# Bias rows added on VectorE, one DMA of rows per chunk, and a new order of work in a fused attention and MLP kernel

## The chip, the cores and the metric

The kernel runs on one core of a Trainium2 chip. The metric is device time in microseconds (us) of one launch; the smaller the better. The core has several engines that run their own instruction streams: TensorE (PE in the profile; PEld is its weight load), VectorE (DVE), ScalarE (ACT), GpSimd (POOL) and SyncE (SP). SyncE, ScalarE and GpSimd also issue DMAs. Every engine works through its instructions strictly in the order in which the program gives them, and waits where an instruction needs something that is not there yet.

## The reference

One input `x` of 2048 rows and 640 columns (bf16) is normalised, and the result goes through two independent branches whose outputs are added to `x`:

```python
xn = layernorm(x)
# A: 32 heads of 20; each position attends to itself and 7 earlier ones, 2 apart
q, k, v = split(xn @ wqkv)
logits = sum_d(q[s] * k[s - 2*w]) * 20**-0.5          # w = 0..7, masked before the start
o = sum_w(softmax(logits)[s, w] * v[s - 2*w]) @ wo
# B: MLP with 1536 hidden units
h = gelu(xn @ w1 + b1) @ w2 + b2
out = x + o + h
```

The change is about the terms `x` and `b2` of the last line, and about the order in which everything is done.

## The kernel before

**Tiling.** The 2048 rows are 16 blocks of 128 (numbers 0 to 15) in 4 chunks of 512 rows (n = 0 to 3; a block has the number bl = 0 to 3 in its chunk). A chunk goes through these stages, each of which is a `do_...` function that issues the instructions of one task:

- `st`, `rs`, `rc`, `xn` (lines 373 to 410): statistics and normalisation of a block, then `tp` and `tc` (412 to 424): transposition on TensorE and a copy to SBUF.
- `pj`/`pc` (438, 475): q, k and v of a chunk, TensorE and a cast on ScalarE. Chunk 0 does this by block with `gj`/`gc`.
- `qk` (488): products q times shifted k on VectorE, eight of 128x2560 elements. `lg` (500): TensorE sums them over a head.
- `m`, `mx`, `ex`, `ss`, `ri`, `at` (525 to 567): the softmax, VectorE and one exponential on ScalarE.
- `xd` and `xs` (569 to 581): the "expansion". The softmax weights `attn`, one row per head, are spread by DMA over the partitions into the tile `ax`, two DMAs issued by SyncE and two by ScalarE.
- `av` (584): eight products v times weights (`pv`) on VectorE; `ad` and `ot` add them up to the tile `oT`.
- `f1`/`ge` (606, 618): the hidden layer, TensorE and the GELU on ScalarE, into 12 tiles `hT`.
- `o` (626): the output of one block, in five pieces `pc` 0 to 4: four of three hidden tiles each, and a last one with `oT` and `wo`. Each weight tile is used for 512 columns into the PSUM tile `lo` and 128 columns into `hi`. Chunks 0 to 2, and blocks 12 and 14 of the last chunk, use one PSUM pair that only one block can hold; blocks 13 and 15 use two of the four `acc` tiles.
- `oc` (647): two casts on ScalarE to the bf16 tile `osb`, of which there are two.
- `od` (653): the block goes to the output by a DMA that GpSimd issues.

**x and b2.** Line 328 loads `b2` into every partition (`b2bc`). Line 330, in SyncE's queue behind all loads, copies the first 15 blocks of `x` from DRAM to the output in DRAM. For each of these blocks `od` then issues two DMAs on GpSimd's queue that add to what the output holds: `b2bc` (line 656) and the computed block (657). The first kind of all blocks runs right after the copy.

Block 15 (`LASTB`) has no such addition. `xb` (426) adds `b2bc` to its rows of `x_sb` on VectorE, and `o` adds the result with a matmul against the identity (line 637). Its 512 wide columns are done first ("lo" only, in five pieces), then cast by `oclo` and stored by a plain DMA of SyncE (666). `ohi` (668) does the 128 narrow columns with 18 matmuls; `ochi` (672) casts on VectorE, and ScalarE issues the store (675).

**The order.** Nothing above is issued in the order of the loops. `make_plan` (149) adds each task with an engine, an assumed duration, a rank, what it needs, the buffers that it holds and, for some, an earliest time. `Plan.run` (57) then walks through time: when an engine is free it takes, among the tasks that are ready and whose buffers fit, the one with the lowest rank. The tasks are issued in the order of their start times in that walk, and this is the order of every engine's stream. The rank is worked out from the chunk (`base` is 52 n, and `early` is `base` - 85, or - 37 for chunk 1), plus the offset of its name in the table `RANK` (141), which is looked up by the first three letters of the name, four for names with "pj", "pc" and "ad". A lower rank goes first. The durations and the walk are assumptions of the program; on the chip the engines take as long as they take, in that fixed order.

The rank of block bl of chunk n is `base` + 60 + 8 bl, and that of `ohi` is 156 + 142 = 298, each plus its offset.

Of the kernel before, what the change touches and what calls it, by code (L numbers as in the profile page):

```python
# [11 lines left out]
ALU = mybir.AluOpType  # L12
# [3 lines left out]
PE, VE, SE, DQ = "pe", "ve", "se", "dq"  # L16


class Plan:
# [101 lines left out]
S, D, F, H, W, DIL = 2048, 640, 1536, 32, 8, 2  # L121
P = 128
DH = D // H
PAD = (W - 1) * DIL
KT, FT = D // P, F // P
CH = 512
NCH = S // CH
BPC = CH // P
# [5 lines left out]
LASTB = S // P - 1  # L134
# [4 lines left out]


RANK = {
# [4 lines left out]
}  # L146


def make_plan(fns, offsets=RANK):

    pl = Plan(offsets)
# [6 lines left out]
    def f(kind, *a):  # L158
        return lambda: fns[kind](*a)

    def done(n, which):
        if n:
            return [f"pc{n}{which}{to}" for to in range(KT)]
        return [f"gc{bl}{g}" for bl in range(BPC) for g, parts in enumerate(GROUPS) if which in [p[0] for p in parts]]

    for n in range(NCH):
        base = n * PERIOD
        prev = base - PERIOD
        early = base + (-37.0 if n == 1 else -85.0)
# [11 lines left out]
            pl.add(f"rc{n}", VE, 0.25, early + -4.0, [f"rs{n}"], f("rstd", n, 0, BPC))  # L181
        for bl in range(BPC):
            xn, tp = ("xn", n, bl), ("acc", "tp", n, bl)
            pl.add(f"xn{n}{bl}", SE if n else VE, 0.65 if n else 0.42, early + -4.0 if n else -99, [f"rc{n}" if n else f"rc{n}{bl}"], f("xn", n, bl), [xn])
            pl.add(f"tp{n}{bl}", PE, 0.3, early + -3.0 if n else -99, [f"xn{n}{bl}"], f("tp", n, bl), [xn, tp])
            pl.add(f"tc{n}{bl}", SE, 0.65, early + -3.0 if n else -99, [f"tp{n}{bl}"], f("tc", n, bl), [tp, xnT])
        if n == NCH - 1:
            pl.add("xb", VE, 0.5, base + 36, [f"xn{n}{BPC - 1}"], f("xb"), after=31.0)

        if n == 0:  # L190
            for bl in range(BPC):
                for g, parts in enumerate(GROUPS):
                    ps, last = ("acc", "g", bl, g), max(p[0] for p in parts)
# [5 lines left out]
        for which, buf in enumerate((q, k, v)):  # L199
# [5 lines left out]
            if which:  # L205
                need = done(n - 1, which) if n else []
# [3 lines left out]
        L = ("L", n)  # L210
        for wp in range(W // 2):
            pr = ("prod", "qk", n, wp)
            for i in range(2):
                need = done(n, 0) + done(n, 1) + [f"pad{n}1"]
                pl.add(f"qk{n}{wp}{i}", VE, 1.42, base + 3.0 * wp + i, need, f("qk", n, wp, i), [q, k, pr])
            pl.add(f"lg{n}{wp}", PE, 0.6, n - 1000, [f"qk{n}{wp}{i}" for i in range(2)] + ([f"lg{n}{wp-1}"] if wp else []), f("lg", n, wp), [pr, L], slack=0.8)

        e, at, ax = ("e", n), ("attn", n), ("ax", n)
        m, rs, ss, z = ("m", n), ("rs", n), ("ss", n), ("prod", "z", n)
# [4 lines left out]
        pl.add(f"ri{n}", VE, 0.96, n - 1000, [f"ss{n}"], f("recip", n), [ss, rs])  # L224
        pl.add(f"at{n}", VE, 1.22, n - 1000, [f"ri{n}"], f("attn", n), [e, rs, at])
        pl.add(f"xs{n}", SE, 1.2, n - 1000, [f"at{n}"], f("xs", n), [at, ax])
        pl.add(f"xd{n}", DQ, 5.5, n - 1000, [f"at{n}"], f("xd", n), [at, ax])

        prs = [("prod", "av", n, wp) for wp in range(W // 2)]
        for wp in range(W // 2):  # L230
            for i in range(2):
                need = [f"xd{n}", f"xs{n}", f"pad{n}2"] + done(n, 2)
                pl.add(f"av{n}{wp}{i}", VE, 1.42, base + 15.0 + 6.0 * wp + i, need, f("av", n, wp, i), [v, ax, prs[wp]])
        for k2, (a, b, r) in enumerate(((0, 1, 9.0), (2, 3, 21.0), (0, 2, 22.0))):
            need = [f"av{n}{x}{i}" for x in (a, b) for i in range(2)] if k2 < 2 else [f"ad{n}0", f"ad{n}1"]
# [8 lines left out]
        for bl in range(BPC):  # L244
            ob = ("osb", n, bl)
            O = [("O", n, bl)] if n < NCH - 1 or bl % 2 == 0 else [("acc", "lo", n, bl), ("acc", "hi", n, bl)]
            final = n * BPC + bl == LASTB
            last = None
            for pc in range(5):
                need = [last] if last else [f"ge{n}{ft}" for ft in range(FT)] + (["xb"] if (n, bl) == (NCH - 1, BPC - 1) else [])  # L250
                if pc == 4:
                    need.append(f"ot{n}")
                us = (0.65, 0.65, 0.65, 0.87, 1.08)[pc] if final else (0.82, 0.82, 0.82, 0.82, 1.37)[pc]
                last = pl.add(f"o{n}{bl}{pc}", PE, us, base + PERIOD + 8.0 + 8.0 * bl, need, f("o", n, bl, pc, ("lo",) if final else ("lo", "hi")), O + (hTs if pc == 0 else hTs[3 * pc : 3 * pc + 3] if pc < 4 else [oT]), 31.0)
            if final:
                pl.add("oclo", SE, 0.55, base, [last], f("oclo"), O + [ob])
                last = pl.add("ohi", PE, 1.05, base + PERIOD + 90, [last], f("ohi"), O)
                pl.add("ochi", VE, 0.25, base, [last], f("ochi"), O + [ob])
                continue
            pl.add(f"oc{n}{bl}", SE, 0.78, base, [last], f("oc", n, bl), O + [ob])  # L260
            pl.add(f"od{n}{bl}", SE, 0.0, base, [f"oc{n}{bl}"], f("od", n, bl), [ob])
# [4 lines left out]
def kernel(  # L266
# [16 lines left out]
    nc = tc.nc  # L283
    assert tuple(A_x.shape) == (1, S, D) and tuple(B_w1.shape) == (D, F)

    x_sd = A_x.rearrange("b s d -> (b s) d")
    out_sd = out.rearrange("b s d -> (b s) d")
# [18 lines left out]
    x_sb = wts.tile([P, NCH * BPC, D], BF16, name="x_sb")  # L306
# [5 lines left out]
    b2bc = consts.tile([P, D], BF16, name="b2bc")  # L312
# [9 lines left out]
    for n in range(1, NCH):  # L322
        cs = slice(n * BPC, (n + 1) * BPC)
# [2 lines left out]
    nc.sync.dma_start(w2_sb[:], B_w2.rearrange("(t p) n -> p t n", p=P))  # L326
    nc.sync.dma_start(wo2[:], A_wo.rearrange("(p t) n -> p t n", t=KT))  # L327
    nc.sync.dma_start(b2bc[:], b2_bcast)  # L328

    nc.sync.dma_start(out_sd[0 : LASTB * P, :], x_sd[0 : LASTB * P, :])  # L330


    ident = consts.tile([P, P], BF16, name="ident")
# [89 lines left out]
            tiles["tp", n, bl][:, 0 : KT * P].rearrange("p (t m) -> p t m", t=KT),  # L423
        )

    def do_xb():
        nc.vector.tensor_tensor(out=x_sb[:, LASTB, :], in0=x_sb[:, LASTB, :], in1=b2bc[:], op=ALU.add)


    def qkv_tile(n, which):  # L430
# [222 lines left out]
    def do_od(n, bl):  # L653
        b = n * BPC + bl
        rows = out_sd[b * P : (b + 1) * P, :]
        nc.gpsimd.dma_start(rows, b2bc[:], accum_op=ALU.add)  # L656
        nc.gpsimd.dma_start(rows, tiles["osb", n, bl][:], accum_op=ALU.add)  # L657


    last = (NCH - 1, BPC - 1)  # L660
# [18 lines left out]
    with tc.manual_schedule(engines=engines):  # L679

        idle = psA.tile([P, CH], F32, tag="acc", name="idle")
        for _ in range(WARM):
            nc.tensor.matmul(idle[:, 0:P], lhsT=ident[:], rhs=ident[:], start=True, stop=True)
        for t in make_plan(fns).run():
            t["fn"]()
# [30 lines left out]
```

## Time and profile before

| | us |
|---|---|
| median of 3 runs | 227.08 |
| lowest and highest run | 226.92 and 228.39 |
| the profiled execution | 227.29 |
| its span, first to last instruction | 225.0 |
| TensorE busy in it | 212.4 |
| VectorE busy | 175.3 |
| ScalarE busy | 115.7 |
| GpSimd busy | 27.8 |

How to read the profile's lines. A line of the timeline has the start, the duration (both us, from the span's start), the engine, the line of the kernel, the operation, the tiles (result <- operands), the shapes and how many instructions are put together; in brackets stands how long the engine was idle before it and what ended that. An engine name with a q behind it is that engine's issuing of a DMA or its semaphore work. In a line of the slices, the span is cut into 40 equal parts, and each digit is the busy share in tenths. A line of the groups has the count, the busy time in us and the mean duration in ns, then the idle time before. A line of the DMA issues has the size of one and the time from issue to landing. A line of one source line's instructions has lowest, median and highest duration in ns, and the first and the last start.

### The profile page before, as it was taken

How to read it: one execution, taken by the hardware profiler on the slowest of the kernel's cores; microseconds unless marked ns; L12 is line 12 of the kernel's file. 1: busy time of each engine (PE TensorE's matmuls, PEld its weight loads, DVE VectorE, ACT ScalarE, POOL GpSimd, SP SyncE). 2: the span in 40 equal slices, each digit the busy share in tenths (PEclk: the TensorE clock that was granted, in tenths of full speed). 3: DMA queues.
4: the chain of work that ended last, by engine and by line, in shares of the span. 5: the costliest groups of instructions: out<-in, count | busy, mean ns of one | idle time of the engine just before them, and what ended most of it. 6: DMA issues, size and time to landing. Idle time of an engine off the chain costs nothing.

```text
span 225.0 us, 4057 instructions
## 1 busy us (share of the span) xinstructions
PE 212.4 (94%) x1728; PEld 123.2 (55%) x1754; DVE 175.3 (78%) x166; ACT 115.7 (51%) x203; POOL 27.8 (12%) x48
## 2 busy tenths in 40 slices
PE   6899999999996999999999999999999999999990
PEld 6799745555443555555555555555445455455550
DVE  3759997567399998999899999999998229995000
ACT  3675988887674746923277542221548431511220
POOL 2000004990000000101010001111100110101111
PEclk9999999999999999999999999999999999999998
DMA  6999992999300000227001422222200532202322
GB/s 228 366 368 389 378 468 42 155 171 198 92 0 0 3 0 0 32 39 179 0 3 26 97 92 29 29 32 31 32 0 0 109 110 29 29 3 29 54 29 35
DMA packets 13625, 21.98 MB, mean 98 GB/s; under 512 B 1144, under 2 KB 10744, under 8 KB 13560
## 3 DMA queue, kind: packets, MB, share of 16 engines
q1 hardware_dynamic: 7848, 14.52, 19.7%
q0 software_dynamic: 4320, 4.92, 16.9%
q10 hardware_dynamic: 1440, 2.29, 3.2%
q8 instruction: 13, 0.21, 0.4%
q14 instruction: 4, 0.03, 0.0%
HBM read 12.45 MB, written 7.54 MB: 89 GB/s over the span
## 4 chain that ended last, share of the span: by engine, by line
issue 71%; POOL 10%; SPq 9%; DMA 7%; POOLq 1%
DMA out_dram<-in_A_x_dram 7%; POOL out_dram L657 5%; POOL out_dram L656 5%; SPq L327 4%; SPq L324 2%; SPq L326 1%; SPq L325 1%; SPq L318 1%; SPq L321 0%; POOLq L711 0%; SPq L320 0%; SPq L328 0%; SPq L315 0%; POOLq L657 0%; POOLq L656 0%
## 5 line engine op out<-in xcount | busy, mean ns | idle before, releaser
L610 PE MATMUL hps<-xnT,w_sb 128*128 128x512 bf16 x234 | 55.2, 380 | 0.3
L588 DVE TENSOR_TENSOR pv<-vT,ax 128x2560 bf16<-128x2560 bf16 x32 | 45.9, 1485 | 12.2 <-DMA ax<-attn 12.1
L643 PE MATMUL lo<-w_sb,hT 128*128 128x512 bf16 x183 | 52.2, 380 | 0.0
L493 DVE TENSOR_TENSOR prod<-qT,kT 128x2560 bf16<-128x2560 bf16 x32 | 45.8, 1486 | 3.1 <-ACT kT L478 2.8
L621 ACT ACTIVATE hT<-hps,b1T 128x512 bf16<-128x512 f32 x48 | 31.9, 688 | 19.7 <-PE hps L610 14.4
L645 PE MATMUL hi<-w_sb,hT 128*128 128x128 bf16 x192 | 40.3, 219 | 0.6 <-issue 0.2
L610 PEld LDWEIGHTS <-w_sb 128*128 128x128 bf16 x240 | 22.4, 98 | 26.2 <-issue 1.5
L597 DVE TENSOR_TENSOR pv<-pv 128x5120 bf16<-128x5120 bf16 x12 | 33.8, 2822 | 0.2
L657 POOL DMA_DIRECT2D out_dram<-osb x15 | 12.9, 863 | 157.0 <-ACT osb L651 157.0
L650 ACT CAST osb<-lo 128x512 bf16<-128x512 f32 x15 | 8.8, 587 | 45.6 <-PE hi L645 29.6
L643 PEld LDWEIGHTS <-hT 128*128 128x128 bf16 x192 | 18.7, 98 | 22.5 <-issue 0.4
L643 PE MATMUL lo<-wo,oT 128*128 128x512 bf16 x76 | 22.4, 380 | 0.0
L645 PEld LDWEIGHTS <-hT 128*128 128x128 bf16 x192 | 18.3, 98 | 2.1
L656 POOL DMA_DIRECT2D out_dram<-b2bc x15 | 13.5, 2696 | 35.1 <-DMA out_dram<-in_A_x_dram 35.1
L443 PE MATMUL pps<-xnT,wq_sb 128*128 128x512 bf16 x72 | 17.5, 381 | 0.2
L443 PE MATMUL pps<-xnT,wk_sb 128*128 128x512 bf16 x74 | 17.3, 379 | 0.2
L645 PE MATMUL hi<-wo,oT 128*128 128x128 bf16 x80 | 16.9, 219 | 0.2
L443 PE MATMUL pps<-xnT,wv_sb 128*128 128x512 bf16 x72 | 16.7, 380 | 0.3 <-ACT xnT L421 0.2
L478 ACT CAST qT<-pps 128x512 bf16<-128x512 f32 x15 | 8.8, 588 | 11.5 <-PE pps L443 11.5
L505 PE MATMUL L<-prod,head_of 128*32 128x256 bf16 x320 | 11.7, 275 | 2.1 <-DVE prod L493 2.1
L376 DVE BATCH_NORM_STATS2 stats<-x_sb 128x6 f32<-128x320 bf16 x16 | 7.4, 462 | 7.1 <-DMA x_sb<-in_A_x_dram 7.1
L399 ACT ACTIVATE xn<-x_sb,nmr,rstd 128x640 bf16<-128x640 bf16 x12 | 10.8, 921 | 4.0 <-PE tp L417 4.0
(68 smaller groups left out, 217.2 us busy)
## 6 DMA issues: line engine op xcount, KB each, us to landing
w_sb<-in_B_w_dram SPq DMA_DIRECT2D x2, 1920.0 KB, 16.4
out_dram<-in_A_x_dram SPq DMA_DIRECT2D x1, 2400.0 KB
out_dram<-b2bc POOLq DMA_DIRECT2D x15, 160.0 KB, 7.3
out_dram<-osb POOLq DMA_DIRECT2D x15, 160.0 KB, 3.4
ax<-attn SPq DMA_DIRECT2D x8, 256.0 KB, 5.3
ax<-attn ACTq DMA_DIRECT2D x8, 256.0 KB, 6.6
x_sb<-in_A_x_dram SPq DMA_DIRECT2D x3, 640.0 KB, 11.4
wq_sb<-in_A_wqkv_dram SPq DMA_DIRECT2D x1, 800.0 KB, 4.7
```

The source lines that it names most:

```text
L399: nc.scalar.activation(xn[:], x_sb[:, b, :], ACT.Identity, bias=nmr[:, b : b + 1], scale=rstd[:, b : b + 1])
L443: nc.tensor.matmul(ps[:], lhsT=wqkv_p[which][:, ti, to, :], rhs=xnT[:, ti, :], start=(ti == 0), stop=(ti == KT - 1),)
L493: nc.vector.tensor_tensor(out=prod[:, i, :, :], in0=qkv_tile(n, 0)[:], in1=qkv_tile(n, 1)[:, :, off : off + CH], op=ALU.mult,)
L505: nc.tensor.matmul(L[j * H : (j + 1) * H, 2 * wp : 2 * wp + 2, :], lhsT=head_of[:], rhs=prod[:, :, t, j * P : (j + 1) * P], start=(t == 0 ...
L588: nc.vector.tensor_tensor(out=pv[:, i, :, :].rearrange("p t (j c) -> p t j c", j=BPC), in0=qkv_tile(n, 2)[:, :, off : off + CH].rearrange( ...
L597: nc.vector.tensor_tensor(out=ta[:], in0=ta[:], in1=tb[:], op=ALU.add)
L610: nc.tensor.matmul(ps[:], lhsT=w1_sb[:, ti, ft * P : (ft + 1) * P], rhs=tiles["xnT", n][:, ti, :], start=(ti == 0), stop=(ti == KT - 1),)
L621: nc.scalar.activation(hT[:], tiles["hps", n, ft][:], ACT.Gelu_apprx_tanh, bias=b1T[:, ft : ft + 1], scale=1.0)
L643: nc.tensor.matmul(lo[:], lhsT=lhs, rhs=rhs[:, 0:CH], start=first, stop=last)
L645: nc.tensor.matmul(hi[:, 0 : D - CH], lhsT=lhs, rhs=rhs[:, CH:D], start=first, stop=last)
L656: nc.gpsimd.dma_start(rows, b2bc[:], accum_op=ALU.add)
L657: nc.gpsimd.dma_start(rows, tiles["osb", n, bl][:], accum_op=ALU.add)
```

## The change

1. The copy of `x` to the output (line 330) is removed, and so is the accumulating DMA of `b2bc` in `od` (line 656).
2. `xb` is now a task of every chunk: one VectorE addition of `b2bc` to the chunk's four blocks of `x_sb`, in place, then one DMA on SyncE's queue that writes these rows to the output (for the last chunk without block 15). It needs the chunk's normalised blocks, and every output block of the chunk needs it in the plan. GpSimd's remaining accumulating DMA adds the computed block to these rows.
3. The plan's durations of `xn`, `lg` and `xd` are raised, and `RANK` is another table, and so the order of all engines is another.

```diff
 RANK = {
-    "ad01": -51.8, "ad02": -11.1, "ad22": 55.2, "av0": -75.4, "av1": -80.6, "av2": 15.4, "f10": 39.3, "f11": 0.8,
-    "f12": 46.1, "f13": 9, "ge1": -74.9, "gj3": 24.7, "o00": 64.8, "o01": 58, "o02": 58.8, "o21": 9.1,
-    "o30": 13.6, "o32": -88, "o33": -87.4, "pc10": 184.3, "pc12": -37.1, "pj21": -29.9, "qk1": -33.9, "qk2": -278.2,
-    "qk3": -4, "st2": 95.7, "tc1": -44.4, "tp2": 50.9, "tp3": -44.5, "xb": 57, "xn1": 17.4, "xn2": 19.4,
+    "av0": 264.6, "av1": 32, "f10": -2, "f11": 10.6, "f12": 127.1, "f13": 83.2, "gj2": -18.9, "gj3": -1.6,
+    "o00": 26.6, "o02": 3.7, "o03": -5.9, "o22": 138.2, "o33": 95.3, "pad": 1.2, "pj22": 202, "pj32": 66.6,
+    "qk2": 13.5, "rc3": 115.5, "st2": 183.2, "tc1": -1, "tp3": -99.8, "xb3": 226, "xn2": 124, "xn3": 8.8,
 }
...
-            pl.add(f"xn{n}{bl}", SE if n else VE, 0.65 if n else 0.42, early + -4.0 if n else -99, [f"rc{n}" if n else f"rc{n}{bl}"], f("xn", n, bl), [xn])
+            pl.add(f"xn{n}{bl}", SE if n else VE, 0.81 if n else 0.42, early + -4.0 if n else -99, [f"rc{n}" if n else f"rc{n}{bl}"], f("xn", n, bl), [xn])
...
-        if n == NCH - 1:
-            pl.add("xb", VE, 0.5, base + 36, [f"xn{n}{BPC - 1}"], f("xb"), after=31.0)
+        pl.add(f"xb{n}", VE, 1.43, base + 36, [f"xn{n}{bl}" for bl in range(BPC)], f("xb", n), after=32.0)
...
-            pl.add(f"lg{n}{wp}", PE, 0.6, n - 1000, [f"qk{n}{wp}{i}" for i in range(2)] + ([f"lg{n}{wp-1}"] if wp else []), f("lg", n, wp), [pr, L], slack=0.8)
+            pl.add(f"lg{n}{wp}", PE, 0.65, n - 1000, [f"qk{n}{wp}{i}" for i in range(2)] + ([f"lg{n}{wp-1}"] if wp else []), f("lg", n, wp), [pr, L], slack=0.8)
...
-        pl.add(f"xd{n}", DQ, 5.5, n - 1000, [f"at{n}"], f("xd", n), [at, ax])
+        pl.add(f"xd{n}", DQ, 6.0, n - 1000, [f"at{n}"], f("xd", n), [at, ax])
...
-                need = [last] if last else [f"ge{n}{ft}" for ft in range(FT)] + (["xb"] if (n, bl) == (NCH - 1, BPC - 1) else [])
+                need = [last] if last else [f"ge{n}{ft}" for ft in range(FT)] + [f"xb{n}"]
...
-    nc.sync.dma_start(out_sd[0 : LASTB * P, :], x_sd[0 : LASTB * P, :])
...
-    def do_xb():
-        nc.vector.tensor_tensor(out=x_sb[:, LASTB, :], in0=x_sb[:, LASTB, :], in1=b2bc[:], op=ALU.add)
+    def do_xb(n):
+        cs = slice(n * BPC, (n + 1) * BPC)
+        nc.vector.tensor_tensor(
+            out=x_sb[:, cs, :],
+            in0=x_sb[:, cs, :],
+            in1=b2bc[:].unsqueeze(1).to_broadcast([P, BPC, D]),
+            op=ALU.add,
+        )
+        cs = slice(n * BPC, min((n + 1) * BPC, LASTB))
+        nc.sync.dma_start(out_sd.rearrange("(b p) d -> p b d", p=P)[:, cs, :], x_sb[:, cs, :])
...
     def do_od(n, bl):
         b = n * BPC + bl
         rows = out_sd[b * P : (b + 1) * P, :]
-        nc.gpsimd.dma_start(rows, b2bc[:], accum_op=ALU.add)
         nc.gpsimd.dma_start(rows, tiles["osb", n, bl][:], accum_op=ALU.add)
```

## The prediction

> **What bounds the kernel now.** I read the page's busy times and slices first, then who waited for whom, then the timeline of the two places where TensorE is idle.
>
> ```profile
> PE 212.4 (94%) x1728; PEld 123.2 (55%) x1754; DVE 175.3 (78%) x166; ACT 115.7 (51%) x203; POOL 27.8 (12%) x48
> PE   6899999999996999999999999999999999999990
> DVE  3759997567399998999899999999998229995000
> ```
>
> TensorE is busy for 212.4 of 225.0 us. Counted from 0, only slices 0 and 1, slice 12 (67.5 to 73.1 us) and slice 39 are under nine tenths. So a change pays by the time at which TensorE ends, or by what follows that. The profiled execution took 227.29 us, 2.26 more than its span; the median of the runs is 227.08, 0.2 lower.
>
> The end of the timeline, then the landing times of the outputs and the closing instructions:
>
> ```profile
> 209.13 1.24 PE L643 MATMUL lo<-wo,oT 128*128 128x512 bf16 x5
> 210.46 0.59 ACT L665 CAST osb<-lo 128x512 bf16<-128x512 f32 x1 [0.38 <-ACT osb L651]
> 211.07 0.35 SPq L666 DMA_DIRECT2D out_dram<-osb  x1
> 213.20 0.38 PE L643 MATMUL lo<-w_sb,hT 128*128 128x512 bf16 x1
> 217.82 0.83 PE L645 MATMUL hi<-w_sb,hT 128*128 128x128 bf16 x12
> 218.54 0.44 PE L645 MATMUL hi<-wo,oT 128*128 128x128 bf16 x5
> 218.57 0.59 ACT L650 CAST osb<-lo 128x512 bf16<-128x512 f32 x1 [3.82 <-DMA out_dram<-osb]
> 219.06 0.27 ACT L651 CAST osb<-hi 128x128 bf16<-128x128 f32 x1
> 219.08 0.29 DVE L674 CAST osb<-hi 128x128 bf16<-128x128 f32 x1 [13.47 <-PE hi L645]
> 219.40 0.36 ACTq L675 DMA_DIRECT2D out_dram<-osb  x1
> 219.62 0.86 POOL L657 DMA_DIRECT2D out_dram<-osb  x1 [3.71 <-ACT osb L651]
> ...
> out_dram<-osb POOLq DMA_DIRECT2D x15, 160.0 KB, 3.4
> out_dram<-osb SPq DMA_DIRECT2D x1, 128.0 KB, 3.1
> out_dram<-osb ACTq DMA_DIRECT2D x1, 32.0 KB, 1.5
> ...
> L711 POOLq EVENT_SEMAPHORE  x4: 17/17/17, 224.3 to 224.9; - x4
> L711 POOLq DRAIN  x3: 40/102/4652, 219.6 to 224.8; - x3
> L711 SPq DRAIN  x3: 7/7/13, 223.5 to 224.5; - x3
> ```
>
> TensorE ends at T = 218.54 + 0.44 = 218.98, and 6.05 us follow. The matmuls end with block 12 (213.20 to 217.8, 4.62 us) and the 17 + 1 narrow ones of block 15's last 128 columns. Block 15's first 512 columns were stored long before (211.07). Block 12's cast, though, waited for an output buffer until 218.57, so its accumulating DMA was issued only at 219.62, to land 3.4 later at 223.0. SyncE's drain follows at 223.5, but GpSimd's own drain (4.65 from 219.6) ends at 224.25, and 0.75 of semaphores close the span. The last output is thus a slow one: GpSimd's, and 0.7 of its drain.
>
> The other idle place, on TensorE and on VectorE before it:
>
> ```profile
> 69.83 0.73 PE L505 MATMUL L<-prod,head_of 128*32 128x256 bf16 x20 [2.06 <-DVE prod L493]
> ...
> 59.87 8.50 DVE L588 TENSOR_TENSOR pv<-vT,ax 128x2560 bf16<-128x2560 bf16 x6 [4.11 <-DMA ax<-attn]
> 68.29 1.48 DVE L493 TENSOR_TENSOR prod<-qT,kT 128x2560 bf16<-128x2560 bf16 x1
> ...
> ax<-attn SPq DMA_DIRECT2D x8, 256.0 KB, 5.3
> ...
> out_dram<-b2bc POOLq DMA_DIRECT2D x15, 160.0 KB, 7.3
> ax<-attn SPq DMA_DIRECT2D x2, 256.0 KB, 8.7
> ax<-attn ACTq DMA_DIRECT2D x2, 256.0 KB, 10.0
> ```
>
> TensorE waits 2.06 us for the last qk product of chunk 1. VectorE had it queued behind six pv products, which had waited 4.11 us for the expansion of chunk 0's weights. The last three rows are the DMA view between 36 and 60 us: with the bias accumulates in flight this expansion took 8.7 and 10.0, against 5.3 as SyncE's median over all chunks.
>
> **The change part by part.**
>
> *What is taken away.* The copy of x into the output and 15 of 30 GpSimd DMAs go.
>
> ```profile
> 21.58 0.67 SPq L330 DMA_DIRECT2D out_dram<-in_A_x_dram  x1
> 21.58 14.83 DMA out_dram<-in_A_x_dram
> 37.05 13.49 POOL L656 DMA_DIRECT2D out_dram<-b2bc  x15 [35.09 <-DMA out_dram<-in_A_x_dram]
> 22.50:31.00 8.50, 8.45 (x95) 5.38 (x94) 8.39 (x11) 8.11 (x17) 0.00 (x0) 1.00 1.20 458
> 31.00:45.00 14.00, 13.89 (x126) 7.63 (x127) 10.26 (x17) 12.13 (x18) 7.96 (x12) 1.00 0.69 141
> ```
>
> By themselves they are worth 0: in the two windows that hold the copy and most of the accumulates, TensorE (first busy column) works 8.45 of 8.50 and 13.89 of 14.00 us. Indirectly the accumulates delayed the expansion, and so made part of the 2.06.
>
> *What VectorE gets.* Four adds of 128x2560 in place of one of 128x640.
>
> ```profile
> L603 DVE TENSOR_TENSOR oT<-pv 128x2560 bf16<-128x2560 bf16 x4 | 5.9, 1486 | 0.1
> L427 DVE TENSOR_TENSOR x_sb<-x_sb,b2bc 128x640 bf16<-128x640 bf16 x1 | 0.5, 486 | 0.0
> 174.87 1.23 DVE L562 TENSOR_TENSOR attn<-e,rs 128x1024 bf16<-128x1024 bf16 x1
> 184.13 5.70 DVE L588 TENSOR_TENSOR pv<-vT,ax 128x2560 bf16<-128x2560 bf16 x4 [8.03 <-DMA ax<-attn]
> 204.12 1.49 DVE L603 TENSOR_TENSOR oT<-pv 128x2560 bf16<-128x2560 bf16 x1
> ```
>
> 4 x 1.49 - 0.49 = +5.5 us. An add has no deadline before its chunk's output blocks, and VectorE has idle time: 8.03 us ahead of chunk 3's pv alone. With rank 156 + 36 + 226 = 418, chunk 3's add comes after all other VectorE work that is ready, so it suits that gap. If the gaps did not cover them, the slack is this: chunk 3's oT is ready at 205.6 with 13.4 us of TensorE work left. The least that must follow oT is about 9.6: pc 4 of blocks 12 and 13 (5/17 of 4.62 each, 2.7), block 14 whole (4.6, since it shares its PSUM pair with block 12), and block 15's last five wide and 18 narrow matmuls (1.1 + 1.2). VectorE may slip 3.8 us against the old end, and 1.7 against an end that is 2.06 earlier, before TensorE waits. I take 0; the bounds are 0 and 5.5.
>
> *What SyncE's queue gets.* Four DMAs of rows, three of 640 KB and one of 480 KB (block 15 is left out). The nearest row for their length is the old copy, 14.83 for 2400 KB, so 3.95 for 640 KB as an upper bound, as that one also read DRAM. Each waits for its add with later expansions behind it; the add stands earlier in VectorE's order, so SyncE loses only the issue, 0.67 us or so. An expansion behind one could be 3.4 late (8.7 against 5.3), or not at all. I take 0 on TensorE, because of the slack above. The Trainium skill (DMA: Bandwidth & Descriptors, section "Queues, rings and completion order") says that a DMA's semaphore increment lands only after all earlier writes of that DMA engine, whichever queue they came from. By that rule rows issued just ahead of an expansion hold it up for their whole length, against this change. The trace agrees as far as the slow first expansion goes, and by the rule the sum would be up to 2 us higher. GpSimd's accumulate now waits for its chunk's rows instead of the bias accumulate; these land long before, as they need only x and its norm.
>
> *The order.* The ranks decide. Before, chunk 3's blocks had rank 229.6 (block 12), 224, 144 and 152.6 (block 15), so block 12 ended last. Now they have 216, 224, 232 and 335.3, with "ohi" at 298 behind block 15's own first columns. Nothing else of TensorE is higher: chunk 3's f1 ends at 156 + 10 + 11 + 83.2 = 260.2. So block 15 ends the work, and it has plain stores. Its wide part ends at T - 1.0, the cast starts 0.1 later (as 210.46 after 210.37) and takes 0.59, SyncE issues at T - 0.3, and this lands 3.1 later: T + 2.8. The narrow part lands as now, at 219.40 + 1.5, which is T + 1.9. Block 14's accumulate is issued at T - 4.1 if block 15 runs whole behind it, or T - 1.2 if only its tail does; GpSimd's drain then ends by T - 1.2 + 4.65 = T + 3.45. From the last landing it is 0.5 to SyncE's drain and 0.75 to the end. End = T + 2.8 + 1.25 = T + 4.05, or T + 4.2 by GpSimd. I take T + 4.1 against T + 6.05 now: -1.95. If the 128 KB land as fast as the 32 KB, it is T + 1.9 + 1.25 = T + 3.15: -2.9. If they land late behind the accumulate beside them, by as much as the expansion was (3.4), it is T + 7.5, +1.4.
>
> *The wait at 67.8.* The ranks of chunk 0's pv go from 15 - 75.4 to 15 + 264.6, behind chunk 1's qk products (52 to 62). So TensorE's product no longer stands behind six pv. I take -2.06 in full; the bounds are -2.06 and a new wait of the size by which the planner misses an expansion: it now books 6.0, chunk 3's took 8.03, so 2.0 at each of perhaps two places, 0 to +2 net. The planner's other new durations change only the order.
>
> Sum: 227.29 - 1.95 - 2.06 = 223.3 us, which I give for the median too, as 0.2 is less than the terms are good for.
>
> **Rivals.**
> A. Only the tail is gained: an expansion is later than booked and makes a new wait of about 2 us on TensorE. For it: 8.03 against 6.0. Against: the present order also booked too little, and chunk 3's TensorE work still hid it. 227.29 - 1.95 = 225.3.
> B. Slower, with VectorE as the bound. All adds (+5.5) and a held-up expansion (+3) lie ahead of chunk 3's oT: 205.6 + 8.5 + 9.6 = T 223.7, end 227.8, time 230.1. It decides above 3.8 us of slip. Against: 8 us of idle time in that very stretch. For: VectorE has nine tenths in nearly all slices from 16 to 29.
> C. The change does not do what it says. Block 15 ends the matmuls, but its 128 KB land behind block 14's accumulate, and the wait on TensorE stays in another place: 227 +- 0.7.
>
> **How the numbers follow.** The forecast has 0.47 (222.2 to 224.4), A 0.28 (224.3 to 226.5), C 0.13, B 0.12. The range 222.2 to 227.2 leaves out B, part of C, and a little below. One per cent, about what a measurement here can tell from no change, is 224.8 and 229.35. Faster by more than that: 0.47 and 0.10 of A, 0.57. Slower: 0.10 of B. Within: the rest, 0.33.
>
> **What would show it.** Right: block 15's casts are the last work, the last GpSimd DMA is issued before T, and the span ends 4 us after TensorE; no TensorE wait over 1 us between 10 us and T; T near 216.9; four adds of 1.49 in VectorE's idle time. Wrong: a wait of TensorE on oT or prod, an expansion of over 8 us with rows beside it, or an end more than 5 us after T.

## The result, and the profile after

| | before | after |
|---|---|---|
| median of 4 runs, us | 227.74 | 221.06 |
| lowest and highest | 226.92, 230.62 | 220.79, 221.94 |
| the profiled execution, us | 227.29 | 220.88 |
| its span | 225.03 | 219.06 |
| TensorE ends at (T) | 218.98 | 215.80 |
| from T to the end of the span | 6.05 | 3.26 |
| outside the span | 2.26 | 1.82 |

The ratio is 0.9725, 95% interval 0.967 to 0.9781: faster by 2.2 to 3.3%. The ratio leaves out the run of 230.62 us, a slow one. The time lies below the predicted range of 222.2 to 227.2. The profiled execution is 6.41 us shorter: 3.18 by T, 2.79 behind it, 0.44 outside the span.

The page after: busy times, then the 40 slices of TensorE and VectorE.

```profile
PE 211.9 (97%) x1728; PEld 123.4 (56%) x1754; DVE 180.4 (82%) x169; ACT 114.6 (52%) x203; POOL 14.5 (7%) x33
PE   7899999999999999999999999999999999999994
DVE  3858999985999999999999999966999999962000
```

Slice 12, which showed the wait before, is full. The last slice of TensorE now holds four tenths, as less comes after the matmuls. VectorE has 5.1 us more work, about the predicted 5.5.

The end of the timeline, the DMA issues, and the closing instructions of the kernel after:

```profile
213.28 0.86 POOL L661 DMA_DIRECT2D out_dram<-osb  x1 [3.75 <-ACT osb L656]
214.87 0.58 ACT L669 CAST osb<-lo 128x512 bf16<-128x512 f32 x1 [1.89 <-issue]
215.36 0.44 PE L650 MATMUL hi<-wo,oT 128*128 128x128 bf16 x5
215.49 0.35 SPq L670 DMA_DIRECT2D out_dram<-osb  x1
215.89 0.29 DVE L678 CAST osb<-hi 128x128 bf16<-128x128 f32 x1 [14.05 <-PE hi L650]
216.21 0.36 ACTq L679 DMA_DIRECT2D out_dram<-osb  x1
...
ax<-attn SPq DMA_DIRECT2D x8, 256.0 KB, 4.6
out_dram<-x_sb SPq DMA_DIRECT2D x3, 640.0 KB, 3.2
out_dram<-osb SPq DMA_DIRECT2D x1, 128.0 KB, 1.7
out_dram<-osb ACTq DMA_DIRECT2D x1, 32.0 KB, 1.5
...
L715 POOLq DRAIN  x3: 34/102/3939, 213.3 to 218.6; - x3
L715 SPq DRAIN  x3: 7/7/13, 218.0 to 218.3; - x3
```

Block 15 ends the work. GpSimd's last DMA is issued at 213.28, 2.5 us ahead of T, and its drain is over at 217.2, so it no longer closes the span. The last to land is the narrow store, 216.21 + 1.5 = 217.7, T + 1.9. The 128 KB store was issued at T - 0.3, as worked out, but landed in 1.7 us where the sum had 3.1. The 160 KB accumulate ahead of that store landed in 3.3 us, at 216.6, and the store 0.6 us behind it.

The adds on VectorE, and what is around chunk 0's expansion (timeline of the kernel after):

```profile
34.91 1.48 DVE L425 TENSOR_TENSOR x_sb<-x_sb,b2bc 128x2560 bf16<-128x2560 bf16 x1
36.76 1.49 DVE L425 TENSOR_TENSOR x_sb<-x_sb,b2bc 128x2560 bf16<-128x2560 bf16 x1 [0.37 <-ACT xn L395]
51.96 11.31 DVE L498 TENSOR_TENSOR prod<-qT,kT 128x2560 bf16<-128x2560 bf16 x8 [2.65 <-ACT kT L483]
63.19 2.88 DVE L593 TENSOR_TENSOR pv<-vT,ax 128x2560 bf16<-128x2560 bf16 x2
78.21 1.48 DVE L425 TENSOR_TENSOR x_sb<-x_sb,b2bc 128x2560 bf16<-128x2560 bf16 x1
142.56 1.48 DVE L425 TENSOR_TENSOR x_sb<-x_sb,b2bc 128x2560 bf16<-128x2560 bf16 x1
200.35 1.49 DVE L608 TENSOR_TENSOR oT<-pv 128x2560 bf16<-128x2560 bf16 x1 [5.01 <-PE hi L650]
```

Two adds stand where VectorE would wait for chunk 0's logits, and the last stands ahead of chunk 3's. All eight qk products of chunk 1 run ahead of chunk 0's first pv, which has no wait before it. Chunk 3's last sum waits 5 us for TensorE to free `oT`: VectorE is early, not late.

Two things had to be told apart. One theory, "O", says that the new order brings the gain, since it takes the qk products out from behind the pv that wait, and puts block 15 last. The other, "D", says that the new path of the rows brings it, since the bias accumulates no longer delay the first expansion. Then the parts of the gain that the sum did not have were to be found: about 0.8 us behind T, and 1.1 at T.

### The profile page after: what moved, and what is told of

Read it like the earlier page. It is cut to its first block, busy times and chain, and to the rows that moved or that the text cites. A ratio compares the mean times of both kernels' runs of the same rounds, so it can differ in the third digit from the quotient of the medians.

```text
span 219.1 us, 4040 instructions
## 1 busy us (share of the span) xinstructions
PE 211.9 (97%) x1728; PEld 123.4 (56%) x1754; DVE 180.4 (82%) x169; ACT 114.6 (52%) x203; POOL 14.5 (7%) x33
## 4 chain that ended last, share of the span: by engine, by line
PE 95%; DVE 1%; DMA 1%; issue 1%; ACT 0%; DVEq 0%
PE lo L648 26%; PE hps L615 23%; PE pps L448 22%; PE hi L650 8%; PE gps L465 8%; PE L L510 5%; PE tp L413 2%; DMA x_sb<-in_A_x_dram 1%; DVE stats L372 0%; DVE stats L373 0%; ACT xnT L417 0%; DVE xn L399 0%; DVE mv L374 0%; DVE osb L678 0%; PE L L520 0%
## 5 line engine op out<-in xcount | busy, mean ns | idle before, releaser
L615 PE MATMUL hps<-xnT,w_sb 128*128 128x512 bf16 x232 | 53.9, 379 | 0.3
L626 ACT ACTIVATE hT<-hps,b1T 128x512 bf16<-128x512 f32 x48 | 31.3, 688 | 15.0 <-PE hps L615 12.5
L648 PE MATMUL lo<-wo,oT 128*128 128x512 bf16 x79 | 23.0, 380 | 0.0
L448 PE MATMUL pps<-xnT,wv_sb 128*128 128x512 bf16 x72 | 17.4, 380 | 0.3 <-issue 0.2
L448 PE MATMUL pps<-xnT,wq_sb 128*128 128x512 bf16 x75 | 16.7, 379 | 0.0
L448 PE MATMUL pps<-xnT,wk_sb 128*128 128x512 bf16 x72 | 16.5, 379 | 0.2
L648 PEld LDWEIGHTS <-oT 128*128 128x128 bf16 x80 | 7.8, 98 | 9.7 <-issue 0.6
L448 PEld LDWEIGHTS <-wq_sb 128*128 128x128 bf16 x75 | 8.7, 117 | 7.2
L448 PEld LDWEIGHTS <-wk_sb 128*128 128x128 bf16 x75 | 8.7, 117 | 7.2
L395 ACT ACTIVATE xn<-x_sb,nmr,rstd 128x640 bf16<-128x640 bf16 x12 | 11.4, 952 | 1.5 <-PE tp L413 1.5
```

Source lines behind the costliest of these rows:

```text
L395: nc.scalar.activation(xn[:], x_sb[:, b, :], ACT.Identity, bias=nmr[:, b : b + 1], scale=rstd[:, b : b + 1])
L448: nc.tensor.matmul(ps[:], lhsT=wqkv_p[which][:, ti, to, :], rhs=xnT[:, ti, :], start=(ti == 0), stop=(ti == KT - 1),)
L615: nc.tensor.matmul(ps[:], lhsT=w1_sb[:, ti, ft * P : (ft + 1) * P], rhs=tiles["xnT", n][:, ti, :], start=(ti == 0), stop=(ti == KT - 1),)
L626: nc.scalar.activation(hT[:], tiles["hps", n, ft][:], ACT.Gelu_apprx_tanh, bias=b1T[:, ft : ft + 1], scale=1.0)
L648: nc.tensor.matmul(lo[:], lhsT=lhs, rhs=rhs[:, 0:CH], start=first, stop=last)
```

## The experiments

In the tables, "T - s" is from TensorE's first projection matmul (at 7.39 before, 7.51 after) to T. It takes out the start, where the projection begins between 7.4 and 7.9 us. "Tail" is from T to the end of the span. The ratio is to the kernel before on the same chip. For reference: before has T - s 211.59 and tail 6.05; after has 208.29 and 3.26.

### The order alone, and the rows alone

The order alone (`e1_order_only`) is the kernel after with the old path of the rows:

```diff
+    nc.sync.dma_start(out_sd[0 : LASTB * P, :], x_sd[0 : LASTB * P, :])
...
     def do_xb(n):
+        if n == NCH - 1:
+            nc.vector.tensor_tensor(out=x_sb[:, LASTB, :], in0=x_sb[:, LASTB, :], in1=b2bc[:], op=ALU.add)
...
+        nc.gpsimd.dma_start(rows, b2bc[:], accum_op=ALU.add)
         nc.gpsimd.dma_start(rows, tiles["osb", n, bl][:], accum_op=ALU.add)
```

> The order of the changed kernel with the rows handled as before: the copy of x in DRAM, the 15 bias accumulates on GpSimd, one VectorE add for block 15 alone. Theory O (the order does it): VectorE does all qk products of chunk 1 ahead of chunk 0's pv, so the slow first expansion (8.7 and 10.0 us in the profile of before) delays nothing, TensorE ends at 215.8 +- 0.5 and the span ends 3.3 us later, near 219; time 220.8 to 221.6. Theory D (the data path does it): with the accumulates back, the first expansion takes 9 to 10 us again, VectorE waits 4 us for it and TensorE 2 us behind it; TensorE ends at 218 or later, time 223 or more.

The rows alone (`e2_data_only`) is the kernel before with the copy and the accumulate removed and `do_xb(n)` of the change. The last add stays where it was in the plan, and the others are put in behind tasks of the old order:

```diff
+        adds = {"qk031": (0, 1), "ot0": (2,)}
         for t in make_plan(fns).run():
             t["fn"]()
+            for n in adds.get(t["name"], ()):
+                do_xb(n)
```

> The order of the kernel before, with the rows handled as in the changed kernel: no copy, no bias accumulates, four VectorE adds with a DMA of rows each, put in behind chunk 0's qk products (chunks 0 and 1), behind chunk 0's oT (chunk 2) and where the single add stood (chunk 3). Theory O: the first expansion lands in 5 to 6 us, the 4.11 us wait of pv for it goes, and with it most of TensorE's wait of 2.06; the end of the order stays, with 6 us after TensorE. Time 225.0 to 226.0, that is 1.5 to 2.5 under before. Theory D: TensorE also gets the other 1.1 us and the shorter tail; time 223 or less. Third case: VectorE's added 5.5 us are felt, time 227.5 or more.

| | time, us | ratio (95%) | T | T - s | tail |
|---|---|---|---|---|---|
| order alone | 221.61 | 0.9747 (0.9677 to 0.9817) | 216.06 | 208.29 | 3.24 |
| rows alone | 224.15 | 0.9854 (0.9795 to 0.9912) | 216.76 | 209.17 | 5.42 |

The order alone has nearly all of the gain, with 30 GpSimd DMAs as before. The DMA view from 36 to 62 us and the waits of that run:

```profile
out_dram<-b2bc POOLq DMA_DIRECT2D x15, 160.0 KB, 7.5
ax<-attn SPq DMA_DIRECT2D x2, 256.0 KB, 9.0
ax<-attn ACTq DMA_DIRECT2D x2, 256.0 KB, 9.7
...
DVE pv L587 <- DMA ax<-attn: 0.2, 1, 0.2
```

The first expansion is as slow as it was before, and VectorE waits only 0.2 us for it. Theory O holds. But the rows alone also remove the wait: T - s falls by 2.42, and the time, 224.15 us, lies below the 225.0 to 226.0 expected by theory O and above the 223 of theory D. Each of the two is enough, and together they do not add. So neither theory is right if it claims the wait for itself alone.

### Without the accumulates

The kernel before without line 656 (`e10_no_accumulates`).

```diff
-        nc.gpsimd.dma_start(rows, b2bc[:], accum_op=ALU.add)
```

> The kernel before without the 15 bias accumulates on GpSimd, and nothing else changed: the copy of x in DRAM and the order stay. It leaves b2 out of the first 15 blocks of the output. Theory X (the accumulates in flight delay chunk 0's expansion, pv waits for it, the qk product waits behind pv, and TensorE behind that): the expansion lands in 5 to 6 us instead of 8.7 to 10, TensorE's wait near 67.8 us goes, TensorE ends at 216.8 as in the run with the new data path in the old order, and the times lie close together near 224.2, against the 226.7 to 230 of the kernel before. Rival (the copy, or the place of the adds in VectorE's order, made the difference in that run): the wait of about 2 us stays, time 227 or more.

Measured: 224.91 us (224.53 to 225.49), ratio 0.9853 (0.977 to 0.9937), T 217.09, T - s 209.19, tail 5.29. Its DMA view from 36 to 60 us and VectorE's timeline:

```profile
ax<-attn SPq DMA_DIRECT2D x2, 256.0 KB, 4.8
ax<-attn ACTq DMA_DIRECT2D x2, 256.0 KB, 5.9
...
52.75 4.30 DVE L493 TENSOR_TENSOR prod<-qT,kT 128x2560 bf16<-128x2560 bf16 x3 [3.60 <-ACT kT L478]
56.97 8.50 DVE L588 TENSOR_TENSOR pv<-vT,ax 128x2560 bf16<-128x2560 bf16 x6
65.38 1.49 DVE L493 TENSOR_TENSOR prod<-qT,kT 128x2560 bf16<-128x2560 bf16 x1
```

The expansion takes a little over half of the 8.7 and 10.0 us that it took before, pv follows the products with no wait, TensorE's wait for the qk product is gone, and T - s is within 0.02 of the rows alone. Theory X holds: the accumulates made the expansion late, and that made TensorE's wait. The copy and the place of the adds have no part in it. The Trainium skill (DMA: Bandwidth & Descriptors, section "Queues, rings and completion order") says that a DMA's completion lands only behind earlier writes of the same DMA engine, from any queue; 8.7 us before against 4.8 here agrees with that, though plain sharing of the engines would look the same here.

### The last blocks

`e3_tail_only` is the kernel before with only the last blocks' ranks changed, `e4_tail_back` the kernel after with only these put back:

```diff
-    "o30": 13.6, "o32": -88, "o33": -87.4,
+    "o33": 95.3,
```

```diff
-    "o33": 95.3,
+    "o30": 13.6, "o32": -88, "o33": -87.4,
```

> The kernel before with the ranks of the last four blocks as in the changed kernel; only TensorE's and ScalarE's orders of these blocks differ from before, so that block 15 ends the work. By the sum of the prediction the tail after TensorE goes from 6.05 to 4.1 us; by the profile of the changed kernel, to 3.3. TensorE's end stays at 219.0 with its wait of 2.06. Time 227.1 - 1.9 = 225.2, or 227.1 - 2.8 = 224.3. Rival: the tail is shorter only in the changed kernel, because its queues have less to finish; then 226.5 to 227.5.

> The changed kernel with the ranks of the last four blocks as before, so that block 12 and its accumulating DMA end the work. Theory O: the tail is 6.0 us again, TensorE's end stays at 215.8; time 221.1 + 2.8 = 223.9 (223.4 to 224.4). Rival: the tail stays under 4.5 us, because GpSimd's queue has only half as many DMAs to close; then 222.3 or less.

`e8_data_and_tail` is the rows alone with the first of these edits.

> The order of the kernel before with the rows handled as in the changed kernel, and the ranks of the last four blocks as in the changed kernel. If the parts add, the tail goes from 5.42 to 3.25 and TensorE's end stays at 216.8, so the time is 224.15 - 2.2 = 222.0; what then is left to the changed kernel, about 1 us, is the rest of its order. If chunk 3's oT comes too late for this order of the last blocks, as in the run with the ranks of the last blocks alone, where TensorE waited 0.99 us for it, it is 223.0.

| | time, us | ratio (95%) | T | T - s | tail |
|---|---|---|---|---|---|
| e3, last blocks new | 227.33 | 0.9946 (0.9907 to 0.9986) | 219.74 | 212.12 | 3.23 |
| e4, last blocks old | 225.81 | 0.9913 (0.9876 to 0.995) | 216.72 | 209.11 | 7.33 |
| e8, rows and last blocks | 222.83 | 0.9759 (0.9705 to 0.9814) | 217.45 | 209.92 | 3.06 |

The tail belongs above all to the last blocks' order: 3.1 to 3.3 with block 15 last, over 5 without. In the old order it is partly paid back: blocks that come earlier need `oT` earlier, and chunk 3's is not ready. These are two rows of the waits of e3, and then one of e8:

```profile
PE lo L643 <- DVE oT L603: 1.0, 1, 1.0
PE pps L443 <- ACT vT L478: 0.7, 1, 0.7
```

```profile
PE lo L650 <- DVE oT L610: 0.6, 1, 0.6
```

So the gain of e3 (1.2 us by the ratio) is less than either figure expected, 1.9 and 2.8. The second row of e3 is no part of its edit: there, one issue of the first expansion on ScalarE took 3.0 us instead of 0.9, and the cast behind it came late. TensorE then reached the qk product later and waited only 0.62 us for it, against 2.06 before. This trace has one of the two shortest spans of e3's ten runs, 223.0 us; eight have 224.4 or more, and what they lose is not shown.

The rival, that fewer DMAs on GpSimd make the tail short, falls with e3 and with the order alone, which have all 30 of them and tails of 3.23 and 3.24. With the old last blocks it has a small part: with 15 of them the tail is 5.42 (rows alone) and 5.29 (`e10`, where GpSimd's closing drain takes 4.00 us) against 6.05, with a drain of 4.65.

In e4 the tail is longer than it ever was before; a row of its waits, then casts and GpSimd DMAs of its last blocks, from its timeline:

```profile
PE lo L648 <- ACT osb L655: 0.7, 1, 0.7
...
213.42 0.59 ACT L655 CAST osb<-lo 128x512 bf16<-128x512 f32 x1 [3.02 <-DMA out_dram<-osb]
217.93 0.59 ACT L655 CAST osb<-lo 128x512 bf16<-128x512 f32 x1 [3.76 <-DMA out_dram<-osb]
...
214.47 0.86 POOL L661 DMA_DIRECT2D out_dram<-osb  x1 [3.87 <-ACT osb L656]
218.98 0.86 POOL L661 DMA_DIRECT2D out_dram<-osb  x1 [3.65 <-ACT osb L656]
```

Block 12 is done on TensorE ahead of T = 216.72, but its cast waits for an output tile until 217.93: cast 1 us, issue, 3.4 us to land, and only then the next cast. With two tiles, one of them block 15's, the last accumulates run one after the other every 4.5 us, and the last landing, 218.98 + 3.4, hangs on this row of DMAs and not on T. TensorE, too, waits 0.7 us for a cast to free the PSUM pair, which is most of the 0.82 by which T - s is above that of the kernel after. With both, e4 takes 225.81 us where 223.9 was expected.

### Why the 128 KB landed in 1.7 us

`e5_early_15` is the kernel after with two pieces of block 15 ahead of block 14:

```diff
+        order = make_plan(fns).run()
+        name = [t["name"] for t in order]
+        late = [order.pop(name.index(k)) for k in ("o333", "o332")]
+        at = [t["name"] for t in order].index("o320")
+        for t in late:
+            order.insert(at, t)
```

> The changed kernel with two pieces of block 15 (its last six hidden tiles and x) moved ahead of block 14, so that block 14's accumulate is issued about 1 us ahead of block 15's 128 KB store instead of 2.2 us. TensorE's work and its end (215.8) stay. Theory L (the packets of the accumulate and of the store run on the DMA engines at the same time): the 128 KB land in about 3.1 us, as in the kernel before, against 1.7 in the changed kernel, and the tail is 4.1 us against 3.26; time +0.9, about 222.0. Rival: the landing depends on something else of the changed kernel and stays at 1.7; the tail is then set by the closing of GpSimd's queue alone.

Measured: 222.20 us, ratio 0.9734 (0.9678 to 0.9789), T - s 208.29, tail 4.31. The end of its timeline, and its output DMAs from 200 us on:

```profile
215.03 0.86 POOL L661 DMA_DIRECT2D out_dram<-osb  x1 [5.26 <-ACT osb L656]
215.73 0.35 SPq L670 DMA_DIRECT2D out_dram<-osb  x1
216.46 0.35 ACTq L679 DMA_DIRECT2D out_dram<-osb  x1
...
out_dram<-osb SPq DMA_DIRECT2D x1, 128.0 KB, 3.0
out_dram<-osb ACTq DMA_DIRECT2D x1, 32.0 KB, 2.5
```

TensorE's time is the same to 0.01 us. With the accumulate 0.7 us ahead of the store instead of 2.2, the store lands in 3.0 instead of 1.7, and the narrow one behind it in 2.5 instead of 1.5. In the kernel before the two were also 0.7 apart (210.37 and 211.07), and it was 3.1. Theory L holds as far as the times go: it is the accumulate in flight, not the store's size. In all three kernels the accumulate was still in flight when the store was issued (it took 3.3 to 3.5 us), and the store landed 0.2 to 0.6 us behind it. Whether the store shares the DMA engines with the accumulate or its completion waits for it, these runs cannot tell.

### What is left at T

With the same rows, the old order has T - s 209.17 and the new one 208.29. No wait of TensorE's matmuls over 0.2 us accounts for these 0.88, nor does the clock: the granted clock is 1.00 up to T in all twelve traces. Nor, by an estimate, is it the last blocks: less its wait of 0.66, e4, which has the old ones, is at 208.45. Two guesses came from the trace. Ahead of a head sum `lg` the weight load is idle for 0.41 us behind 512-column matmuls and for 0.26 behind a block's piece, so the first step costs 0.15 us more (theory S), and the old order has 13 of the dear kind, the new one 8, counted along the weight loads. A piece of a block that follows 512-column work takes 0.975 us against 0.815 (theory E), and there are 18 such entries in the old order, 12 in the new one. All three kernels move tasks in the list of the kernel after:

```diff
+        order = make_plan(fns).run()
+        for task, before in MOVES:
+            at = [t["name"] for t in order]
+            t = order.pop(at.index(task))
+            order.insert([t["name"] for t in order].index(before), t)
```

Here MOVES is, for `e6_wide_first`, `e7_block_first` and `e9_interleaved`:

```
 e6: (o002, f1111) (o003, f1111) (pj322, lg30) (pj220, lg33) (pj300, lg13)
 e7: (o010, lg11) (o011, lg12) (o100, lg21) (o110, lg23) (o120, lg31)
 e9: (o030, f115) (o031, f115) (o020, f117) (o021, f117) (o000, f119) (o002, f1111) (o222, f1311)
```

> The changed kernel with four head sums (lg) on TensorE put behind a projection's 512-column matmuls instead of behind a piece of an output block: the third and fourth... of chunk 1, the first of chunk 2 and two of chunk 3, as far as the data allow it. In both traces the step into a head sum costs 0.30 us behind 512-column matmuls and 0.15 behind an output piece. Theory S (this step cost is the rest of the gain at TensorE's end): TensorE's wait ahead of its head sums goes from 5.1 to about 5.7 us, and TensorE ends 0.4 to 0.6 later, 216.2 to 216.4; time about 221.6. Rival: the step cost is hidden or moved elsewhere; TensorE's end stays at 215.8 +- 0.2.

> The changed kernel with pieces of output blocks put ahead of five head sums on TensorE (two in chunk 1, two in chunk 2, one in chunk 3), three or four of which stood behind 512-column matmuls. Theory S: TensorE's wait ahead of its head sums goes from 5.1 to about 4.5 us, and TensorE ends 0.4 to 0.6 earlier, at 215.2 to 215.4; time about 220.6. Rival: TensorE's end stays at 215.8 +- 0.2, or is later, since the delayed head sums delay VectorE's softmax.

> The changed kernel with five more changes of TensorE from 512-column work (hidden layer) back to a piece of an output block: seven pieces of blocks 3, 2, 0 and 10 are moved ahead of a hidden tile, with no other work added. In the changed kernel's trace a piece that follows such work takes 0.975 us against 0.815 inside a block, and there are 12 such entries against 18 in the order before. Theory E (the entries are what is left of the gain at TensorE's end): 5 x 0.16 = +0.80, TensorE's end 216.6 (time from its first projection to the last narrow matmuls up by 0.8), time 221.9. Rival (the entries are paid back elsewhere, as the head sums' were): TensorE's end stays at 215.8 +- 0.2 and the time at 221.1.

| | time, us | ratio (95%) | T | T - s |
|---|---|---|---|---|
| e6 | 221.69 | 0.9711 (0.9645 to 0.9777) | 216.55 | 208.90 |
| e7 | 220.98 | 0.9688 (0.9627 to 0.9749) | 215.88 | 208.29 |
| e9 | 220.96 | 0.9656 (0.9574 to 0.9737) | 215.90 | 208.30 |

The waits of the weight loads ahead of the head sums, in the rows alone, in the kernel after, in e6 and in e7:

```profile
PEld L512 <- issue: 6.0, 15, 0.4
```

```profile
PEld L510 <- issue: 5.1, 15, 0.4
```

```profile
PEld L510 <- issue: 5.7, 15, 0.4
PEld L413 <- ACT xn L395: 1.0, 3, 0.4
PEld L448 <- issue: 0.9, 4, 0.3
PEld L648 <- DVE oT L608: 0.5, 2, 0.3
```

```profile
PEld L510 <- issue: 4.6, 15, 0.4
```

These rows moved as theory S said, and e6 was slower by the expected amount. But e7, with 0.5 us less in the same row, ends no earlier, and e9 ends within 0.01 us of the kernel after with five more entries. Both guesses fall. What one step costs more, the task beside it costs less: in e9 the hidden tile ahead of an entry takes 0.92 us instead of 1.08, which is the 0.16 that the entry costs more. A task's time here runs from its first weight load to that of the next, so a load that comes early takes from the one task what it gives to the other. The extra 0.6 us of e6 go with new waits for `xn` and `oT` in its other rows; that they are the whole of it was not tried. What makes the 0.88 us between the two orders stays open. The row of the head sums differs by just that, 6.0 against 5.1, but e7 took 0.5 out of this row and gained nothing.

No kernel here beats the changed one clearly: e7 and e9 have 220.98 and 220.96 against its 221.06, whose own runs spread over 1.15.

## Why the prediction was too careful

- **The wait at 67.8.** Taken in full at -2.06: right, and it was -2.40 in T - s when the accumulates alone were taken out; the 0.34 beyond the wait was not traced. Its chain (accumulates, expansion, pv, qk product, TensorE) is shown link by link by e10; that an order with pv behind the products also suffices, by e1. The feared new wait of about 2 us (rival A) did not come.
- **The tail.** "Block 15 ends the work, and it has plain stores", and the issue at T - 0.3: right. The step that failed is "this lands 3.1 later: T + 2.8". The 3.1 came from a row in which the store was issued 0.7 us behind an accumulate, and here the accumulate was 2.2 us ahead. It took 1.7, so the narrow store at T + 1.9 decided. The sum's other end, GpSimd's drain at T + 3.45, failed too: it was over at T + 1.4, as its last DMA was issued at T - 2.5, between the two cases considered (T - 4.1 and T - 1.2). The tail was -2.79, near the lower bound given (-2.9), not -1.95. The price of the overlap was in the row used; the sum did not ask what was in flight there.
- **The order.** The sum priced it at nothing besides the wait and the tail. It gave another 0.9 us. This step was missing altogether, and its cause was not found.
- **The adds and the rows.** Taken as 0, and no cost of theirs shows. Chunk 3's add went ahead of its logits, at 142.56, and not into a gap ahead of its pv, as the sum had it. The rows landed in 3.2 us for 640 KB (bound 3.95), and the expansions in 4.6 as SyncE's median. The trace gave no case of the rule weighed there, as the rows were never just ahead of an expansion. VectorE, the bound of rival B, had 5 us to spare.
- **Outside the span.** 2.26 became 1.82 and was not thought of. It is 1.7 to 1.9 in all but one run of e1, e2 and e4, 2.1 to 2.5 in most runs of the kernel before (up to 3.2 in others), and 2.1 in two runs of e10 and 3.0 in the other two; no part of the change was found that it belongs to.

From 223.3 to the profiled 220.88 it is 2.4: 0.84 in the tail, 0.9 in the order, 0.34 in the wait and 0.44 outside, less 0.12 by which the start was later.

## What to carry to other kernels

When a landing time is taken from a row, look at what else was in flight there; the same store 2.2 us and 0.7 us behind an accumulate differed by 1.3 us. A wait at the end of a chain can be cut at any link, so two edits that each remove it do not add, and only runs with one edit at a time show it. A step that looks dear in a trace may be paid back by its neighbour: move it and look at the end before building on it.

## What the runs showed of the hardware

- The 15 accumulating DMAs of 160 KB nearly doubled the time of a DMA between SBUF tiles on other queues beside them: 8.7 us on SyncE's queue before, 4.8 without them (e10).
- In the kernel after, a plain store of 32 KB landed in 1.5 us, one of 128 KB, 2.2 us behind an accumulate, in 1.7, and 640 KB in 3.2. With the accumulate 0.7 us ahead of the 128 KB store and 1.4 ahead of the 32 KB one (e5), these took 3.0 and 2.5.
- GpSimd's closing drain took 4.65 us from its last DMA before, and so was over 1.2 us after that DMA had landed; after, 3.94, and the stores landed later. It was 4.64 to 4.72 in the kernels with 30 GpSimd DMAs (before, e1, e3) and 3.94 to 4.17 in those with 15.
- The kernel before spread from 226.7 to 230.0 us over 18 runs on one chip, and each kernel without the accumulates or with the new order over 1.7 us at most. In e3, which keeps both causes, the wait for the qk product was 0.62 us in the profiled execution, against 2.06 before, so it varies. Whether this makes the spread was not shown.
